# Each product of a split fp32r matmul as two products of 256 moving columns

## The chip, the cores and the metric

The kernel runs on one core of one Trainium2 chip. The core's engines work side by side, each on its own list of instructions: TensorE (PE in the profile, with its weight loads shown apart as PEld), VectorE (DVE), ScalarE (ACT), GpSimd (POOL) and SyncE (SP), which issues most of the DMAs. TensorE writes its results into PSUM, which the kernel uses as eight banks of 128 partitions by 512 fp32 columns. The metric is the device time of one execution in microseconds (us).

## The reference

One input of 2048 rows and 512 columns goes through four layers, each with a residual: a Fourier mixing layer, an attention layer with a compressive memory, and both once more. Cut to what matters:

```python
x = x + _A_ref(_layernorm(x), dft_seq_re, dft_seq_im, dft_hid_re, dft_hid_im)
x = x + _B_ref(_layernorm(x), wq, wk, wv, wo, beta)
x = x + _A_ref(_layernorm(x), ...)
x = x + _B_ref(_layernorm(x), ...)

def _A_ref(x, Cr, Ci, Wr, Wi):        # y = Real(DFT_seq(DFT_hidden(x)))
    a, b = x @ Wr.T, x @ Wi.T
    return Cr @ a - Ci @ b            # Cr, Ci: 2048 x 2048

def _B_ref(x, wq, wk, wv, wo, beta):  # 32 heads of 16, 4 segments of 512 rows
    q, k, v = x @ wq, x @ wk, x @ wv
    for s in range(4):
        p = softmax(q_s @ k_s.T * scale + mask)          # within the segment, causal
        o_s = g * (phi(q_s) @ M) / (phi(q_s) @ z + 1e-6) + (1 - g) * (p @ v_s)
        M, z = M + phi(k_s).T @ v_s, z + sum(phi(k_s))   # memory for later segments
    return o @ wo
```

All of it is fp32 at its inputs and outputs.

## The kernel before

**Split products.** The large matrix products run in fp32r, a form of fp32 on TensorE. To keep their accuracy, each operand is split into two fp32r tensors: `split` (line 95) rounds the source to `hi` (a copy on ACT, line 99, or on DVE, line 97) and stores the rest, source minus `hi`, as `lo` (on DVE or POOL, line 101). A pair of them lies side by side in one tile of 128 x 2 x 512. `matmul3` (line 107) then adds three products into one PSUM bank: hi times hi, hi times lo and lo times hi. Its stationary operand (`lhsT`) has 128 columns, its moving operand (`rhs`) 512, so one product fills a whole bank. `first` and `last` say whether this call opens or closes the accumulation in the bank.

**Where it is used.** Six places call it, and the profile names their results by their banks:

- `contract` (line 306), banks `u`: the first Fourier layer's transform along the rows. For each of 4 blocks of 512 output columns, 16 chunks of 128 rows are accumulated into 8 banks (4 for the real part and 4 for the imaginary one). Stationary is the normalised input `xa`, moving are the split blocks `chi` and `clo` of the DFT matrix.
- `product` (line 333), banks `m`: the same transform in the second Fourier layer, in a form with seven block products instead of eight (`P1` to `P7`), each summed over 8 chunks into two banks.
- `hidden` and `hidden_last` (lines 372 and 391), banks `y`: the transform along the columns in both Fourier layers, with the split result `us` stationary and the split weights `wdt` moving.
- `proj` (line 500), banks `pqk`, and `values` (line 480), banks `pvv`: the projections to q, k and v of the attention.
- `outproj` and `outproj_split` (lines 860 and 889), banks `po`: the output projection.

Every other product of the attention stays outside `matmul3`: `nat` and `sT` are bf16 scores (of a row maximum and of the softmax), `pv_bank` is the product with the values, `pm` and `pM` read and update the memory, `xnT`, `oT`, `on`, `pkT` and `mT` are transposes.

**The order of work.** Each piece of work is a generator. `place` puts its steps on numbered slots, and at the end all slots are run in order, so the program is written out step by step. All PE instructions go through one helper, `in_order` (line 83, the call itself on line 87), which keeps them in program order; that is why the profile gives line 87 for all of them. The other engines' instructions are ordered by the framework's scheduler, which follows the order of the program but lets an instruction under `tc.high_priority(offset=...)` count as if it stood that many instructions earlier. That is used for DVE's row maxima (`natural_max`, line 602, with `URGENT = 150` of line 41; line 618 with twice that) and for ACT's copy of them (line 640). A row maximum is taken by DVE from a bank `nat` into `mx` (line 603); from four of them come `parts`, which PE transposes (`mT`), and which a DMA then writes into the stack of queries that the products `sT` read.

In the attention stages, runs of a few `matmul3` products stand between the scores of one unit and the next; in the Fourier stages thousands of them follow each other.

Of the kernel before, what the change touches and what calls it, by code (L numbers as in the profile page):

```python
# [61 lines left out]
def spectral_infini_kernel(  # L62
# [13 lines left out]
    V, A, G, T = nc.vector, nc.scalar, nc.gpsimd, nc.tensor  # L76
# [6 lines left out]
    def in_order(engine, name):  # L83
        op = getattr(engine, name)

        def call(*args, **kwargs):
            return tc.keep_in_program_order(op(*args, **kwargs))  # L87

        return call

    T = SimpleNamespace(matmul=in_order(T, "matmul"), transpose=in_order(T, "transpose"))
# [13 lines left out]
            )  # L105

    def matmul3(ps, lhsT, rhs, first, last):
        T.matmul(ps, lhsT(0), rhs(0), start=first, stop=False)
        T.matmul(ps, lhsT(0), rhs(1), start=False, stop=False)
        T.matmul(ps, lhsT(1), rhs(0), start=False, stop=last)  # L110

    def rows(ap, i):
        return ap[i * P : (i + 1) * P, :]
# [76 lines left out]
    def place_spectral(x_in, x_out, t0, end, ln_at, direct):  # L190
# [115 lines left out]
        def contract(tcn):  # L306
            ps = [[bank(f"u{d}") for d in range(DT)] for _ in range(2)]
            for k in range(HALF):
                for h2 in range(2):
                    for cc in range(2):  # L310
                        parts = right[tcn, cc, k]
                        for d in range(DT):
                            matmul3(
                                ps[cc][d],
                                lambda h: xa[k + HALF * h2][:, h, d * P : (d + 1) * P],
                                lambda h: parts[h][:, h2],
                                (k, h2) == (0, 0),
                                (k, h2) == (HALF - 1, 1),
                            )
                        if (k, h2, cc) != (HALF - 1, 1, 1):  # L320
                            yield
            for cc in range(2):
                for d in range(DT):
                    if d % 2 == 0:
                        block(tcn, (d // 2, cc))
                    dst = c[tcn, (d // 2, cc)][:, d % 2]
                    if cc == 0:
                        A.activation(dst, ps[cc][d], AF.Copy)
                    else:
                        V.tensor_scalar(dst, ps[cc][d], -1.0, None, op0=ALU.mult)  # L330
            yield

        def product(tcn, name):
            ps = [bank(f"m{m}") for m in range(2)]
            for k in range(HALF):
                t = right[tcn, name, k]
                for m in range(2):
                    matmul3(
                        ps[m],
                        lambda h: left(name, k, h, m),  # L340
                        lambda h: t[:, h],
                        k == 0,
                        k == HALF - 1,
                    )
                if k < HALF - 1:
                    yield
            for j, base, _ in TERMS[name]:
                if base != j:
                    block(tcn, j)
            for m in range(2):  # L350
                for j, base, op in TERMS[name]:
                    dst = c[tcn, j][:, m]
                    if base is None:
                        A.activation(dst, ps[m], AF.Copy)
                    else:
                        V.tensor_tensor(out=dst, in0=c[tcn, base][:, m], in1=ps[m], op=op)
            yield
# [14 lines left out]
        def hidden(tcn):  # L372
            for tt in range(LT):
                ps = bank("y")
                xr = load_rows(x_in[tcn * LT + tt], "xr")
                for cc in range(2):
                    for d in range(DT):
                        ut, w = us[tcn, tt, cc], wdt[cc, d]
                        matmul3(
                            ps,  # L380
                            lambda h: ut[:, h, d * P : (d + 1) * P],
                            lambda h: w[:, h, :],
                            (cc, d) == (0, 0),
                            (cc, d) == (1, DT - 1),
                        )
                        if (cc, d) != (1, DT - 1):
                            yield
                finish(ps, xr, x_out, tcn * LT + tt)
                yield
# [712 lines left out]
```

## Time and profile before

| | |
|---|---|
| device time, median of 3 runs | 1908.67 us (1908.55 to 1909.09) |
| span of the profiled execution | 1911.1 us |
| PE: busy, matmuls | 1809.7 us (95% of the span), 10336 |
| PEld: busy, weight loads | 1301.0 us (68%), 10336 |
| DVE busy | 1311.1 us (69%) |
| ACT busy | 1062.9 us (56%) |
| POOL busy | 512.5 us (27%) |
| mean granted TensorE clock | 0.985 |

The profiled execution's own time is its span, 2.4 us above the median of the runs. By time it falls into the first Fourier layer (to about 470 us), the first attention layer (to about 980), the second Fourier layer (to about 1400) and the second attention layer; neighbouring layers overlap a little at each border.

How the profile is read: the span runs from the first instruction to the last. Busy time of an engine is the time in which at least one of its instructions runs. For PE that includes the time from a matmul's issue to its last result, and since matmuls overlap each other, the durations of single ones add up to more than the busy time. A row of a group of instructions names the line, engine, operation, tile written and tiles read, shapes and count; then the busy time and the mean duration of one in ns; then the idle time of the engine just before them, and after whom it ended. In the timeline, a row is the start in us from the span's start, the length in us, and how many equal instructions follow each other in it. Matmul rows name the active rows and columns of the array (`128*128`) and then the moving operand (`128x512`).

### The profile page before, as it was taken

The numbers are of one execution on the slowest core, as the hardware profiler recorded it, in microseconds if no ns is written. First come the engines' busy times: TensorE is split into PE (matmuls) and PEld (weight loads), VectorE is DVE, ScalarE is ACT, GpSimd is POOL, SyncE is SP. The second block draws the span as 40 slices with busy tenths as digits, with TensorE's granted clock in tenths as the row PEclk, the third lists the DMA queues.
The fourth block names the chain that finished last, engine by engine and source line by source line (L and its number), as shares of the span: only waits on it lengthen the run. The fifth ranks groups of instructions, "written<-read, shape, count | busy, mean of one in ns | idle before, by whom it ended". The sixth has DMA issues, their size and how long they took to land. (4 is left out here: it accounts for less than half of the span.)

```text
span 1911.1 us, 31877 instructions
## 1 busy us (share of the span) xinstructions
PE 1809.7 (95%) x10336; PEld 1301.0 (68%) x10336; DVE 1311.1 (69%) x4073; ACT 1062.9 (56%) x2292; POOL 512.5 (27%) x831
## 2 busy tenths in 40 slices
PE   7899999999899999999889999999988999999998
PEld 6678888888556656665458888787865655666654
DVE  8654545462787787777866687777558778777773
ACT  3221213331578777767664465453337877777775
POOL 4200000002345344446431000000124443434432
PEclk9999999999899999999999999999999999999998
DMA  6665555353544333434445787563444434444231
GB/s 224 233 208 199 189 191 198 115 173 121 178 125 148 118 120 115 149 119 134 134 154 181 222 251 225 164 204 127 159 150 139 144 108 134 126 133 142 91 117 45
DMA packets 165655, 296.49 MB, mean 155 GB/s; under 512 B 17776, under 2 KB 66928, under 8 KB 165488
## 3 DMA queue, kind: packets, MB, share of 16 engines
q1 hardware_dynamic: 162224, 293.68, 47.5%
q8 instruction: 81, 1.33, 0.3%
q10 hardware_dynamic: 3264, 0.79, 0.2%
q14 instruction: 86, 0.70, 0.1%
HBM read 192.95 MB, written 100.66 MB: 154 GB/s over the span
## 5 line engine op out<-in xcount | busy, mean ns | idle before, releaser
L603 DVE CUSTOM_DVE_ANT_0 junk<-nat,mask 128x512 bf16<-128x512 f32 (+3 forms) x1024 | 496.6, 485 | 203.2 <-PE nat L87 183.9
L669 ACT ACTIVATE pT<-sT 128x512 f32<-128x512 f32 x640 | 370.3, 598 | 15.0 <-ACT sT L668 2.2
L87 PE MATMUL u<-chi,xa 128*128 128x512 f32 x1024 | 321.1, 395 | 10.9 <-DVE xa L97 7.3
L672 POOL TENSOR_SCALAR_AFFINE_SELECT pT<-pT 128x256 f32<-128x256 f32 (+1 forms) x448 | 197.4, 455 | 431.5 <-ACT pT L669 366.8
L87 PE MATMUL sT<-stkq,stkk 99*128 99x256 bf16 (+3 forms) x1024 | 250.7, 307 | 17.5 <-DVE mx L603 8.8
L87 PE MATMUL nat<-stkk,stkq 96*128 96x512 bf16 (+3 forms) x1024 | 246.5, 302 | 20.8 <-DVE mx L603 12.4
L668 ACT ACTIVATE sT<-sT 128x256 f32<-128x256 f32 (+1 forms) x640 | 208.6, 334 | 63.9 <-PE sT L87 56.7
L87 PEld LDWEIGHTS u<-chi,xa 128*128 128x128 f32 x1024 | 195.4, 191 | 52.8 <-issue 7.2
L87 PE MATMUL u<-clo,xa 128*128 128x512 f32 x512 | 202.6, 396 | 9.6 <-DVE clo L101 9.6
L142 POOL TENSOR_TENSOR r<-ve,half_neg 128x2 f32<-128x2 f32 (+1 forms) x33 | 24.0, 728 | 696.5 <-DVE ve L140 692.9
L87 PE MATMUL y<-wdt,us 128*128 128x512 f32 x768 | 182.5, 391 | 1.2 <-DVE wdt L101 1.2
L87 PEld LDWEIGHTS <-stkk 99*128 99x128 bf16 x1024 | 82.6, 99 | 146.3 <-issue 127.9
L87 PEld LDWEIGHTS y<-wdt,us 128*128 128x128 f32 x768 | 143.4, 188 | 31.6 <-DVE wdt L101 2.0
L87 PE MATMUL pv_bank<-pT,vt 128*17 128x128 f32 (+3 forms) x2048 | 158.7, 440 | 1.7 <-POOL pT L672 1.6
L87 PEld LDWEIGHTS <-stkq 96*128 96x128 bf16 x1024 | 94.9, 99 | 75.9 <-issue 37.3
L87 PE MATMUL po<-wo,oh 128*128 128x512 f32 x384 | 125.7, 443 | 7.6 <-DVE oh L101 5.4
L87 PE MATMUL pvv<-wv,xT 128*128 128x512 f32 x384 | 127.0, 443 | 3.9 <-DVE mx L603 3.9
L87 PE MATMUL pqk<-xT,wq 128*128 128x512 f32 x384 | 129.9, 447 | 0.0
L87 PE MATMUL pqk<-xT,wk 128*128 128x512 f32 x384 | 127.8, 442 | 0.0
L87 PEld LDWEIGHTS u<-clo,xa 128*128 128x128 f32 x512 | 97.7, 191 | 32.5 <-DVE clo L101 12.2
L87 PEld LDWEIGHTS pv_bank<-pT,vt 128*17 128x17 f32 x2048 | 57.6, 98 | 90.7 <-issue 77.0
L99 ACT ACTIVATE clo<-cring 128x512 fp32r<-128x512 f32 x112 | 70.6, 631 | 69.1 <-DVE chi L101 37.9
(138 smaller groups left out, 3032.0 us busy)
## 6 DMA issues: line engine op xcount, KB each, us to landing
sum<-sring SPq DMA_DIRECT2D x32, 1024.0 KB
cring<-sum SPq DMA_DIRECT2D x128, 256.0 KB
stkq<-scrq SPq DMA_DIRECT2D x64, 384.0 KB
stkk<-scrk SPq DMA_DIRECT2D x64, 384.0 KB
cring<-in_ct SPq DMA_DIRECT2D x96, 256.0 KB
sring<-in_ct SPq DMA_DIRECT2D x32, 512.0 KB
xt<-mid SPq DMA_DIRECT2D x64, 256.0 KB
craw<-in_ct SPq DMA_DIRECT2D x30, 512.0 KB
```

The costliest lines, as they stand in the source:

```text
L87: return tc.keep_in_program_order(op(*args, **kwargs))
L99: A.activation(hi, src, AF.Copy, scale=scale)
L142: G.tensor_tensor(out=r, in0=ve, in1=half_neg[:, :n], op=ALU.pow)
L603: V.tensor_tensor_reduce(junk[:, :n], src, mask[:, 512 - n :], 1.0, 3e38, ALU.add, ALU.min, dst,)
L668: A.activation(blocks, blocks, AF.Relu)
L669: A.activation(dst, ps, AF.Exp, scale=-SCALE)
L672: G.affine_select(blocks, blocks, pattern=[[0, n] for n in blocks.shape[1:-1]] + [[1, P]], compare_op=ALU.is_ge, fill=0.0, base=0, channel ...
```

## The change

`matmul3` issues each of its three products twice: once on the moving columns 0 to 255 into the first half of the bank, and once on the columns 256 to 511 into its second half, with the same stationary operand. Only the very first product in a bank opens the accumulation, and both halves of the last term close it. Everything else in the program's text is as before; lines below `matmul3` are numbered 8 higher.

```diff
     def matmul3(ps, lhsT, rhs, first, last):
-        T.matmul(ps, lhsT(0), rhs(0), start=first, stop=False)
-        T.matmul(ps, lhsT(0), rhs(1), start=False, stop=False)
-        T.matmul(ps, lhsT(1), rhs(0), start=False, stop=last)
+        terms = (0, 0), (0, 1), (1, 0)
+        for a, b in terms:
+            for c in 0, 256:
+                T.matmul(
+                    ps[:, c : c + 256],
+                    lhsT(a),
+                    rhs(b)[:, c : c + 256],
+                    start=first and (a, b, c) == (0, 0, 0),
+                    stop=last and (a, b) == terms[-1],
+                    skip_group_check=True,
+                )
```

## The prediction

> **What bounds the kernel now.** I read the page first: its line of the span, its table of busy time and its table of DMA queues.
>
> ```profile
> span 1911.1 us, 31877 instructions
> ...
> PE 1809.7 (95%) x10336; PEld 1301.0 (68%) x10336; DVE 1311.1 (69%) x4073; ACT 1062.9 (56%) x2292; POOL 512.5 (27%) x831
> ...
> q8 instruction: 81, 1.33, 0.3%
> ...
> q14 instruction: 86, 0.70, 0.1%
> ```
>
> TensorE (PE) is busy 95% of the span and no other engine passes 69%. A busy share alone does not say where PE sets the pace, so next come the windows by stage. The columns are the window, its length, then busy time and instructions of PE, PEld, DVE, ACT and POOL, then granted clock, DMA share and GB/s.
>
> ```profile
> 0.00:130.00 130.00, 109.48 (x442) 87.32 (x443) 90.89 (x171) 34.72 (x44) 35.07 (x41) 0.96 0.66 224
> 130.00:470.00 340.00, 340.00 (x1510) 281.48 (x1509) 169.58 (x263) 92.06 (x151) 10.91 (x10) 1.00 0.52 175
> 470.00:980.00 510.00, 470.95 (x3223) 295.43 (x3222) 393.43 (x1594) 368.73 (x865) 231.79 (x384) 0.97 0.42 132
> 980.00:1400.00 420.00, 415.40 (x1866) 338.66 (x1865) 284.15 (x514) 198.78 (x364) 25.15 (x28) 1.00 0.59 188
> 1400.00:1911.00 511.00, 473.82 (x3303) 298.12 (x3301) 373.07 (x1533) 368.61 (x869) 209.62 (x369) 0.98 0.38 121
> ```
>
> The spectral stages (130 to 470, 980 to 1400) leave PE idle 0 and 4.6 us. The attention stages leave 39.1 and 37.2 us, the first 130 us leave 20.5. So a time added to each product of a spectral stage reaches the end in full, and in the other stages nearly so. The longest of the waits in the third window is this (total, times, longest):
>
> ```profile
> PE nat L87 <- DVE mx L603: 6.7, 12, 1.6
> ```
>
> It is a loop: DVE takes a maximum of what PE has just made, and PE waits for the bank. Slower products elsewhere on PE give DVE more time for it, but I credit nothing for that.
>
> The products that the change touches are these groups, by form. The columns are names and shapes, count, busy time and mean ns of one, then idle time before.
>
> ```profile
> L87 PE MATMUL u<-chi,xa 128*128 128x512 f32 x1024 | 321.1, 395 | 10.9 <-DVE xa L97 7.3 <-ACT chi L99 3.3 <-POOL xa L101 0.4
> L87 PE MATMUL u<-clo,xa 128*128 128x512 f32 x512 | 202.6, 396 | 9.6 <-DVE clo L101 9.6
> L87 PE MATMUL y<-wdt,us 128*128 128x512 f32 x768 | 182.5, 391 | 1.2 <-DVE wdt L101 1.2
> L87 PE MATMUL pqk<-xT,wq 128*128 128x512 f32 x384 | 129.9, 447 | 0.0
> L87 PE MATMUL pqk<-xT,wk 128*128 128x512 f32 x384 | 127.8, 442 | 0.0
> L87 PE MATMUL pvv<-wv,xT 128*128 128x512 f32 x384 | 127.0, 443 | 3.9 <-DVE mx L603 3.9
> L87 PE MATMUL po<-wo,oh 128*128 128x512 f32 x384 | 125.7, 443 | 7.6 <-DVE oh L101 5.4 <-DVE mx L603 0.9 <-ACT oh L99 0.7
> L87 PE MATMUL m<-chi,xa 128*128 128x512 f32 x384 | 99.8, 396 | 0.0
> L87 PE MATMUL m<-clo,xa 128*128 128x512 f32 x384 | 99.3, 394 | 0.0
> L87 PE MATMUL m<-clo,xb 128*128 128x512 f32 x192 | 49.6, 391 | 1.8 <-DVE clo L101 1.8
> L87 PE MATMUL m<-chi,xb 128*128 128x512 f32 x192 | 48.7, 389 | 0.0
> L87 PE MATMUL m<-chi,xs 128*128 128x512 f32 x96 | 25.1, 393 | 0.0
> L87 PE MATMUL m<-clo,xs 128*128 128x512 f32 x96 | 24.4, 389 | 0.0
> ```
>
> The counts add up to 1536 (u) + 768 (y) + 768 (pqk) + 384 (pvv) + 384 (po) + 1344 (m) = 5184 products. The mean of one (389 to 447 ns) is a latency and not a price, since products overlap. The price is the distance from start to start, read where nothing but such products runs (window, length, busy time and count of PE, granted clock, DMA):
>
> ```profile
> 150.00:350.00 200.00, 200.00 (x884) 1.00 0.56 192
> 55.70:59.50 3.80, 3.80 (x11) 0.50 0.39 126
> ```
>
> The first row gives 200.00 / 884 = 0.2262 us for a product, at a granted clock of 1.00; 5184 of them are 1173 us, 61% of the span. The second is a stretch at clock 0.50, and the timeline there (start, length, count) shows:
>
> ```profile
> 55.61 1.05 PE L87 MATMUL u<-chi,xa 128*128 128x512 f32 x2
> ...
> 58.17 1.05 PE L87 MATMUL u<-chi,xa 128*128 128x512 f32 x2
> ```
>
> Six products start between 55.61 and 58.17 (two, one, two and one, by the three rows left out): 2.56 / 6 = 0.427 us each. Half of that is 0.2133, so at full clock a product takes 0.0129 us more than its array time. At half clock nothing of this excess is left, which is how a supply of moving data that is a little too slow at full clock behaves (it would grow with the columns). But a fixed time for each instruction that a longer product hides would also look so. What the change costs hangs on which of the two it is.
>
> **The change part by part.** It replaces each of 5184 products by two with 256 moving columns, and adds 5184 products and, if none is shared, 5184 weight loads. PE's order is the old one with each product doubled. No wait, transfer, tile or DMA issue is added or removed.
>
> *The products.* No fp32r product of 256 columns stands in the trace, so the price is bounded by rows. The lower end: array time alone, 0.1067 each, would be 0.2133 a product, a gain of 0.0129; the weight loads raise that end (below). The upper end: the whole excess for each half, 0.1067 + 0.0129 = 0.1196, or 0.2391 a product. Between them stand two near rows, of like length and with one weight load each:
>
> ```profile
> 1770.68 0.39 PE L87 MATMUL sT<-stkq,stkk 99*128 99x512 bf16 x1
> 1770.90 0.38 PE L87 MATMUL nat<-stkk,stkq 96*128 96x256 bf16 x2
> ```
>
> ```profile
> 1775.51 0.39 PE L87 MATMUL sT<-stkq,stkk 99*128 99x256 bf16 x2
> 1775.74 0.38 PE L87 MATMUL nat<-stkk,stkq 96*128 96x512 bf16 x1
> ```
>
> The sT pair is this very form in bf16, two products of 256 columns in the halves of one bank: 1775.74 - 1775.51 = 0.23 us, against 1770.90 - 1770.68 = 0.22 for one of 512. The pM products are as long as a half and load weights of the same size (the timeline, then the groups):
>
> ```profile
> 529.52 1.09 PE L87 MATMUL pM<-vt,pkn 128*128 128x136 f32 x8
> ```
>
> ```profile
> L87 PE MATMUL pM<-vt,pkn 128*128 128x136 f32 x192 | 26.7, 282 | 4.9 <-DVE mx L603 4.9
> ...
> L87 PEld LDWEIGHTS pM<-vt,pkn 128*128 128x128 f32 x192 | 24.9, 189 | 7.3 <-ACT sT L668 5.3 <-ACT pT L669 1.1
> ```
>
> Eight in 1.09 us, with the last one's 0.28 taken off, are 0.81 / 7 = 0.116 each. I take 0.1155 for a half, 0.231 for a product, since both rows (0.230 and 0.232 a pair) lie there. That is 0.231 - 0.2262 = +0.0048 us, times 5184 = +24.9 us.
>
> *The weight loads.* Each now has 0.1155 us of product to hide under instead of 0.2262. One load takes 0.19 us from issue to end, but pM shows loads of 189 ns under products 0.116 apart, so loads overlap each other's latency. How close they can stand:
>
> ```profile
> 24.37 0.30 PEld L87 LDWEIGHTS u<-chi,xa 128*128 128x128 f32 x2 [0.85 <-POOL xa L101]
> ```
>
> Two in 0.30 us, the last of them 0.19 long, are 0.11 apart. That is the floor of a half, 0.22 a product (a gain of 0.0062, the lower end kept), and leaves some 5 ns of cover at 0.1155. I cost them at nothing. If the cover is gone by 5 ns a half, it is 2 x 0.005 x 5184 = +52 us, within the upper end of the products.
>
> The Trainium skill (TensorE: Matmul & The Clock Gate, "LDWEIGHTS") puts a load of 128 columns at 128 / 1.2 = 107 ns. The two loads 0.11 us apart agree. By that figure a half would stay at or above 107 ns, which speaks against any large gain.
>
> *Instruction fetch.* Queue q8 holds 1.33 of 1.33 + 0.70 = 2.03 MB of instructions, 66%, as PE and PEld hold 20672 of 31877; it is PE's. 10368 more instructions are 41 packets more. A packet takes 0.3% x 16 x 1911 / 81 = 1.1 us, and 122 instead of 81 make one in 16 us instead of 24. Prefetch hides it; if it hid nothing, +45 us. I take 0.
>
> *Order on other engines.* DVE, ACT, POOL and SP keep their instructions; some move by a few places, because the urgency of DVE's maxima is an offset counted in instructions (URGENT = 150) and now reaches over fewer steps. The bound is the idle PE of the attention stages, 39.1 + 37.2 = 76 us: a third of it more or less is 25 us either way. I take 0.
>
> *Cover in the first 130 us.* Part of PE's 20.5 idle us there is waiting for split inputs, which a slower PE meets later: I take -1 us for its 442 products (442 x 0.0048 = 2.1, half of it).
>
> **Sum.** 24.9 - 1 = +24, so a span of 1911.1 + 24 = 1935 us. The median of the runs, 1908.67, lies 2.4 below the profiled span, so 1932.7, and I say 1933 us, +1.3%. Anything within 0.2% (3.8 us) counts as no change.
>
> **The rivals.**
>
> *The excess belongs to the instruction.* Each half carries 0.0129: +0.0129 x 5184 = +67, with the same -1 us some 1975; with some 10 us more for the shortened cover, 1985. For it: the excess is the same in 884 products in a row, whatever they read. Against it: none of it is left at half clock.
>
> *The other side: the excess is not paid by a short product.* It would have to arise beyond the 256th column; then a half runs as fast as its weight load permits, 0.11, and the kernel gains 0.0062 x 5184 = 32 us: 1877. It decides as soon as a half falls below 0.1131. For it: sT's 512 columns at 0.22 show that 512 columns need not cost 0.226. Against it: the sT pair is slower than one of 512, and pM, with a load of this size, stands at 0.116.
>
> The Trainium skill (same page, "Back-to-back issue gap") gives 518 cycles for 512 columns and 262 for 256 at 2.4 GHz: 216 and 109 ns. By it a pair would take 218 ns, and against the 226 measured here the change would gain 0.0079 x 5184 = 41 us, 1868. Its 216 fits sT's 0.22 and not the fp32r products' 0.226, so I give its side little weight.
>
> *A weight load doesn't fit under a half.* If the products waited for the whole 0.19 us of each load, a product would take 0.38: +0.15 x 5184 = +800 us, 2710. pM speaks against it. A narrow product could also run in a slower form; no row shows one.
>
> *The pair shares one load.* The time would be as forecast, loads being hidden, but PEld would stay near x10336. Against it: the first two products of each three already have one stationary operand, and there are as many loads as products (x10336 each).
>
> **How the numbers follow.** Forecast (a half between 0.1135 and 0.118, 1912 to 1960 us): 0.46. Excess per instruction, with reordering or fetch on top, 1960 to 1990: 0.29. No change: 0.05. Faster: 0.14. Worse than 1990, weight loads above all: 0.06. The range 1905 to 1990 leaves out about 2 in 10, the faster runs and the worst; faster 0.14, same 0.05, slower 0.81.
>
> **What would show it.** Right: PE at about 15520 matmuls and as many loads, windows of a spectral stage with 0.115 us a product, its stages longer by 2% (130 to 470 becoming some 347 us) and PE still without idle there. If the window shows 0.120, the excess is the instruction's; 0.110, the loads set the pace; 0.113, supply alone. The idle PE of the attention stages should stay near 76 us; if it grows by 20 or more, the order of DVE's work matters and I was wrong to cost it at nothing. Doubled latency of q8 packets with idle PE "from issue" would blame the fetch. I am wrong altogether if fp32r products of 256 columns have a rate of their own.

## The result and the profile after

The changed kernel takes 1953.81 us (median; 1944.17 to 1955.68) beside 1908.61 us for the kernel before: 1.0235 times as long, 95% interval 1.0216 to 1.0254. The forecast was 1933, with a range of 1905 to 1990.

The page of the changed kernel begins with its span and the busy times:

```profile
span 1954.0 us, 42263 instructions
...
PE 1859.8 (95%) x15520; PEld 1632.4 (84%) x15520; DVE 1301.8 (67%) x4073; ACT 1062.1 (54%) x2292; POOL 511.3 (26%) x831
...
q8 instruction: 122, 2.00, 0.4%
```

Every product is doubled (10336 + 5184 = 15520) and so is its weight load: nothing is shared within a pair. PE is as full as before, and PEld went from 68% to 84% of the span. The other engines' busy times are what they were.

The rate is in the window from 150 to 350 us, where only these products run. Columns: window, length, then busy time and count of PE, PEld, DVE, ACT and POOL, then granted clock, DMA share, GB/s.

```profile
150.00:350.00 200.00, 200.00 (x1669) 200.00 (x1669) 97.80 (x128) 46.93 (x59) 0.00 (x0) 1.00 0.54 182
```

200.00 / 1669 = 0.1198 us for a half, 0.240 for a product that took 0.2262 before. Such a count also holds the products that reach over the two ends of the window, so these quotients come out up to 0.2% low. The timeline of the kernel before gives the whole product more closely, with three of them from 360.15 to 360.83, 0.2267 each; by their start times the halves stand 0.1200 apart:

```profile
360.15 0.62 PE L87 MATMUL u<-chi,xa 128*128 128x512 f32 x2
360.60 0.39 PE L87 MATMUL u<-clo,xa 128*128 128x512 f32 x1
360.83 0.62 PE L87 MATMUL u<-chi,xa 128*128 128x512 f32 x2
```

The weight loads are busy for all 200 us of the window, where before (the row below) they were for 165.6 of them:

```profile
150.00:350.00 200.00, 200.00 (x884) 165.59 (x883) 103.25 (x135) 49.57 (x62) 0.00 (x0) 1.00 0.56 192
```

The timeline of PEld after the change shows how they stand:

```profile
358.98 0.55 PEld L87 LDWEIGHTS u<-chi,xa 128*128 128x128 f32 x4
359.46 0.31 PEld L87 LDWEIGHTS u<-clo,xa 128*128 128x128 f32 x2
359.70 0.55 PEld L87 LDWEIGHTS u<-chi,xa 128*128 128x128 f32 x4
```

Six loads start from 358.98 to 359.70, 0.120 apart, each still running when the next one starts. By the start times in the trace (medians of the window), a load starts 0.003 us after a product has started, and the load's own product 0.117 us after the load. At granted clock 0.50 nothing is lost, as in the kernel before (four halves in 0.85 us, 0.213 each, where a whole product took 0.427):

```profile
57.61 1.05 PE L87 MATMUL u<-chi,xa 128*128 128x256 f32 x4
58.46 0.63 PE L87 MATMUL u<-clo,xa 128*128 128x256 f32 x2
58.89 1.05 PE L87 MATMUL u<-chi,xa 128*128 128x256 f32 x4
```

Where the time came from shows when both executions are cut at the same products (the last `y` and the first `m` of each layer). First before, then after:

```profile
0.00:484.00 484.00, 463.48 (x2014) 379.32 (x2014) 266.52 (x453) 128.64 (x198) 50.71 (x55) 0.99 0.55 184
484.00:969.70 485.70, 446.65 (x3103) 278.49 (x3101) 381.94 (x1561) 360.99 (x849) 223.06 (x376) 0.97 0.42 133
969.70:1411.20 441.50, 436.90 (x1973) 353.67 (x1972) 294.08 (x540) 206.52 (x380) 33.87 (x36) 0.99 0.58 185
1411.20:1911.10 499.90, 462.62 (x3252) 289.54 (x3251) 368.58 (x1519) 366.75 (x866) 204.89 (x365) 0.98 0.39 122
```

```profile
0.00:504.90 504.90, 487.03 (x4003) 485.03 (x4003) 268.06 (x453) 128.51 (x198) 51.83 (x55) 0.99 0.54 177
504.90:991.90 487.00, 447.63 (x3755) 339.26 (x3753) 376.09 (x1561) 361.12 (x850) 222.38 (x376) 0.97 0.43 132
991.90:1455.30 463.40, 459.92 (x3819) 454.34 (x3817) 293.30 (x540) 205.66 (x379) 33.62 (x35) 0.99 0.58 177
1455.30:1954.00 498.70, 465.22 (x3952) 353.76 (x3950) 364.36 (x1519) 366.79 (x866) 203.52 (x365) 0.98 0.40 123
```

The Fourier stages grew by 20.9 and 21.9 us, the attention stages by 1.3 and -1.2. All but 0.1 of the 42.9 us lies in the Fourier stages, where such products set the pace, although the attention stages gained some 650 and 700 products each.

### The profile page after: what moved, and what is told of

It reads as the page before. It is cut to its first block, busy times and chain, and to the rows that moved or that the text cites. A ratio compares the mean times of both kernels' runs of the same rounds, so it can differ in the third digit from the quotient of the medians.

```text
span 1954.0 us, 42263 instructions
## 1 busy us (share of the span) xinstructions
PE 1859.8 (95%) x15520; PEld 1632.4 (84%) x15520; DVE 1301.8 (67%) x4073; ACT 1062.1 (54%) x2292; POOL 511.3 (26%) x831
## 4 chain that ended last, share of the span: by engine, by line
PE 77%; DVE 11%; issue 4%; DMA 4%; ACT 2%; POOL 1%; SPq 0%; DVEq 0%; ACTq 0%; POOLq 0%
PE u L87 16%; PE m L87 15%; PE y L87 8%; PE pqk L87 7%; PE pv_bank L87 6%; PE sT L87 6%; PE nat L87 5%; DVE junk L611 4%; PE pvv L87 4%; PE po L87 4%; DMA xt<-mid 2%; PE on L87 1%; PE pM L87 1%; PE pm L87 1%; DVE sring L304 1%
## 5 line engine op out<-in xcount | busy, mean ns | idle before, releaser
L87 PE MATMUL u<-chi,xa 128*128 128x256 f32 x2048 | 333.3, 285 | 9.1 <-DVE xa L97 7.6
L87 PEld LDWEIGHTS u<-chi,xa 128*128 128x128 f32 x2048 | 286.1, 194 | 9.4 <-issue 7.6
L87 PE MATMUL u<-clo,xa 128*128 128x256 f32 x1024 | 209.1, 286 | 8.8 <-DVE clo L101 8.8
L87 PE MATMUL y<-wdt,us 128*128 128x256 f32 x1536 | 192.2, 284 | 0.8 <-DVE wdt L101 0.8
L87 PEld LDWEIGHTS u<-clo,xa 128*128 128x128 f32 x1024 | 161.5, 194 | 10.1 <-DVE clo L101 10.1
L87 PE MATMUL pqk<-xT,wq 128*128 128x256 f32 x768 | 134.4, 312 | 0.5 <-ACT vt L504 0.5
L87 PE MATMUL po<-wo,oh 128*128 128x256 f32 x768 | 127.3, 306 | 6.8 <-DVE oh L101 4.2
L87 PE MATMUL pvv<-wv,xT 128*128 128x256 f32 x768 | 131.3, 311 | 2.1 <-DVE mx L611 2.1
L87 PE MATMUL pqk<-xT,wk 128*128 128x256 f32 x768 | 126.8, 302 | 0.0
L87 PEld LDWEIGHTS po<-wo,oh 128*128 128x128 f32 x768 | 105.7, 194 | 18.9 <-DVE oh L101 9.8
```

## The experiments

The trace after leaves two readings of 0.120. The array time of 512 columns at full clock is 0.2133 us, half of the 0.427 measured at clock 0.50, so 2.4 columns pass in a ns. By the first reading, each fp32r instruction carries 0.0133 us beside its columns: 256 / 2.4 + 13.3 = 120 ns, and 512 / 2.4 + 13.3 = 226.7. By the second, the columns come at 17/16 of the array's time (226.7 for 512, 113.3 for 256), and a half waits for its weight load at 120. Both give the same two numbers. The experiments had to part them, and to say why the attention stages paid next to nothing.

**Only the Fourier layers split, only the attention split.** `matmul3` gets a flag that the calls in the attention set.

```diff
+    def matmul3(ps, lhsT, rhs, first, last, attention=False):
+        cuts = ((0, 256), (256, 256)) if attention == False else ((0, 512),)
```

(`attention == True` in the other kernel.)

> Only the Fourier layers' products (u, m, y: 3648) are split, the attention's stay at 512 columns. Theory P (the fixed cost of an fp32r instruction, 0.0133 us at full clock, is paid once more for each product, and PE never waits in these layers): 3648 x 0.0133 = 48 us, less what half clock and the input waits of the first 130 us give back, so +38 to +46 us, about 1950. Rival Q (the measured +45 us spread evenly over all products): 45 x 3648 / 5184 = +32 us, about 1940.

> Only the attention's products (pqk, pvv, po: 1536) are split. Theory P with what the short runs of the kernel before show (about 0.232 us a product there and not 0.2267, so a split adds only some 0.005 to 0.007): +4 to +11 us, 1913 to 1920. Rival Q (even spread): +13 us, 1922. If the order of DVE's maxima cost something, it would show here as more PE idle and +20 us or more.

Splitting the Fourier layers alone gave 1.0239 (1.0205 to 1.0274), the whole of the loss. Splitting the attention alone gave 1.0008 (0.9987 to 1.0029): no change. So the even spread (Q) is refuted, and theory P was near for the Fourier layers (medians 1952.8 against 1907.9, +45). For the attention it expected 4 to 11 us, and the medians differ by +0.7; the interval, -2.5 to +5.5 us, leaves only the lower end of that open. One short run of products in the attention, before and after, shows why little is added there. First before, then after, the same instructions:

```profile
1770.68 0.39 PE L87 MATMUL sT<-stkq,stkk 99*128 99x512 bf16 x1
1770.90 0.38 PE L87 MATMUL nat<-stkk,stkq 96*128 96x256 bf16 x2
1771.04 0.94 PE L87 MATMUL pvv<-wv,xT 128*128 128x512 f32 x3
1771.83 0.39 PE L87 MATMUL sT<-stkq,stkk 99*128 99x512 bf16 x1
```

```profile
1816.12 0.39 PE L87 MATMUL sT<-stkq,stkk 99*128 99x512 bf16 x1
1816.35 0.39 PE L87 MATMUL nat<-stkk,stkq 96*128 96x256 bf16 x2
1816.48 0.96 PE L87 MATMUL pvv<-wv,xT 128*128 128x256 f32 x6
1817.28 0.39 PE L87 MATMUL sT<-stkq,stkk 99*128 99x512 bf16 x1
```

From sT to sT the start times in the trace give 1.150 us before and 1.165 after: 0.005 for a product, and not 0.013. The first of the three takes 0.320 before and 0.319 after. Its load starts only 0.024 us ahead of it in both, so nothing covers that load, and the split adds nothing. The other two go from 0.232 and 0.230 to 0.241 and 0.240. The 467 runs of three in the traces of the kernel before and of the attention split, paired in order, grew by a median of 0.016 us, 5.7 us in all. Why the median of the runs shows even less can't be told from a single execution; PE's waits may have taken up a part.

**The three terms inside, the halves outside.** Neighbours no longer alternate between the halves of the bank.

```diff
-        for a, b in terms:
-            for c in 0, 256:
+        for c in 0, 256:
+            for a, b in terms:
```

> The same six products, but all three terms of the first half of the bank before those of the second, so that two neighbours no longer share a stationary operand in pairs and no longer alternate between the halves. If the cost belongs to each instruction: 0.120 us a product in the window from 150 to 350 us, time as the changed kernel (1944 to 1956). If it comes from going back and forth between the halves of a bank: below 0.115 a half and 20 us or more faster than the changed kernel. If from loading the same weights twice: about the same in the hi-hi and hi-lo terms, so no change either.

1.0213 (1.0188 to 1.0237), and 200.00 us for 1669 halves in the window, as in the changed kernel. The order of halves and of shared stationary operands has no part in it.

**384 and 128 columns.**

```diff
-            for c in 0, 256:
+            for c, n in ((0, 384), (384, 128)):
```

> Each product as 384 and 128 columns. The law that 512 and 256 give (0.0133 us and one column in 1/2.4 ns): the 384 takes 0.1733. For the 128 the law alone gives 0.0667; the weight load, which two in a row show at 0.11, would hold it at 0.107 to 0.11; a load that needs a handover of its own, 0.120. So a pair is 0.240, 0.280 to 0.283 or 0.293. With 5184 products against 0.2267: +69, +277 to +292, or +344 us.

1.151 (1.1463 to 1.1557), some 289 us more. The timeline:

```profile
300.02 0.74 PE L87 MATMUL u<-chi,xa 128*128 128x384 f32 x4
300.60 0.45 PE L87 MATMUL u<-clo,xa 128*128 128x384 f32 x2
300.88 0.74 PE L87 MATMUL u<-chi,xa 128*128 128x384 f32 x4
```

Three products in 0.86 us, 0.287 each, between the 0.283 and the 0.293 expected. So a short product is held back by the load beside it; from this alone the two readings can't be told apart, since 0.170 + 0.117 and 0.173 + 0.113 both fit. The loads start 0.109 and 0.178 us apart in turn, so 0.120 is not the closest that two such loads come while products run.

**Shorter weight loads.** Some terms load only 64 stationary columns, and so fill half of the partitions.

```diff
         for a, b in terms:
+            n = 64 if (a, b) == (0, 1) else P
...
-                    ps[:, c : c + 256],
-                    lhsT(a),
+                    ps[:n, c : c + 256],
+                    lhsT(a)[:, :n],
```

> As the changed kernel, but the hi-lo term loads 64 stationary columns instead of 128 and so fills half of the partitions (the other half of that term is left out). Two of six loads are half as long. If the product's fixed cost doesn't depend on the load: 0.120 a half still, time as the changed kernel. If a half is set by its load of 128 columns and a handover: the two short loads give 0.107 to 0.109 instead of 0.120, a mean of 0.116 in the window, and 20 to 40 us faster.

In the second kernel it is `n = P if (a, b) == (0, 0) else 64`.

> As the changed kernel, but the hi-lo and the lo-hi term load 64 stationary columns (half of each of these terms is left out), so four of six loads are short. If a half is the longer of 0.1133 (its columns) and 0.120 (a load of 128 columns with its handover): (2 x 0.120 + 4 x 0.1133) / 6 = 0.1156 a half in the window from 150 to 350, after 0.1178 with two short loads. If the load doesn't matter: 0.120.

The first gave 1.0128 (1.0092 to 1.0164), about 18 us less than the changed kernel; the second 1925 us in a single run. Their windows, one after the other:

```profile
150.00:350.00 200.00, 200.00 (x1701) 200.00 (x1700) 99.85 (x131) 47.04 (x59) 0.00 (x0) 1.00 0.55 186
```

```profile
150.00:350.00 200.00, 200.00 (x1733) 200.00 (x1732) 101.36 (x133) 48.06 (x60) 0.00 (x0) 1.00 0.57 191
```

0.1176 and 0.1154 us a half, where the second reading gives (4 x 120 + 2 x 113.3) / 6 = 117.8 and (2 x 120 + 4 x 113.3) / 6 = 115.6. The expectation for the first kernel had 0.116, since it put the products with short loads at 0.107 to 0.109; by the second reading their columns hold them at 0.1133. The products still have 256 moving columns in fp32r. With a cost of each instruction they would have stayed at 0.120. So the half of the changed kernel is as long as its weight load permits, and without it would take 0.1133, half of a whole product. The sum of the first reading was right and its mechanism wrong. These two kernels alone leave one doubt: a product with 64 stationary columns also writes only 64 partitions, and might be shorter for that. The next experiment has short loads beside products that write all 128.

**bf16 read from the same tiles.** The operands are the upper halves of the fp32r numbers, so the columns still lie 4 bytes apart; the lower bits are left out of the products.

```diff
-                    lhsT(a),
-                    rhs(b)[:, c : c + 256],
+                    lhsT(a).bitcast(BF16)[:, 1::2],
+                    rhs(b).bitcast(BF16)[:, 1::2][:, c : c + 512],
```

(`c + 256` in the second kernel.)

> All split products read the upper half of each fp32r number as bf16 (every second 2-byte element of the same tiles), 512 columns, one instruction a product, as in the kernel before; this leaves the lower bits out of both operands. If the fixed cost belongs to the fp32r form: 0.2153 to 0.220 us a product in the window 150 to 350 (the bf16 products sT take 0.22), some 30 to 56 us faster than before. If every matmul of 512 columns with such operands pays it: 0.2267, no change.

> The same in bf16, each product as two of 256 columns. If the fixed cost belongs to the fp32r form: 0.108 to 0.110 a half, within 15 us of the run with 512 bf16 columns. If splitting costs the same in every form: 0.120 a half, some 45 us slower than the run with 512 bf16 columns.

With 512 columns 0.9884 (0.9855 to 0.9912), with 256 0.9908 (0.9879 to 0.9937), and 4.6 us between their medians. The windows of the two, 512 first (of its matmuls some records are missing; its 882 loads count the products):

```profile
150.00:350.00 200.00, 198.81 (x866) 84.67 (x882) 103.12 (x135) 49.64 (x62) 0.00 (x0) 1.00 0.57 192
```

```profile
150.00:350.00 200.00, 200.00 (x1767) 169.41 (x1766) 104.13 (x137) 48.61 (x61) 0.00 (x0) 1.00 0.57 191
```

200.00 / 882 = 0.2268 and 200.00 / 1767 = 0.1132. For 512 columns the second price expected came out, without its "no change" in time; for a half neither 0.108 to 0.110 nor 0.120 did. The excess is there in bf16 too, so it isn't a cost of the fp32r form. And it halves with the columns, so it isn't a cost of the instruction. With short bf16 loads (0.10 us from issue to end) a half of 256 columns and all 128 partitions takes 0.1133, which puts what fp32r pays above that on its load, and the split itself is almost free. The 22 us that the kernel with 512 columns gains on the one before, at the same 0.2267 in the long runs, lie mostly in the attention stages, which are 9.5 and 10.6 us shorter in the profiled executions. That they come from the shorter loads at the head of each short run is possible but wasn't tried alone.

**One column read 512 times.** fp32r, unsplit, with step zero in the moving operand; the other 511 columns are left out.

```diff
-        T.matmul(ps, lhsT(0), rhs(0), start=first, stop=False)
...
+            T.matmul(
+                ps,
+                lhsT(a),
+                rhs(b)[:, :1].to_broadcast([P, 512]),
```

> fp32r, 512 columns, one instruction a product as in the kernel before, but the moving operand is its first column read 512 times (step zero), so the result is left out of it. If the 0.0133 us come from how many different bytes are read: 0.2153 to 0.217. If they belong to the fp32r form, whatever it reads: 0.2267.

```profile
150.00:350.00 200.00, 200.00 (x925) 174.86 (x925) 107.00 (x140) 51.20 (x64) 0.00 (x0) 1.00 0.59 197
```

The single run took 1868 us. 200.00 / 925 = 0.2162: nearly all of the excess is gone, with the same form and the same loads. It belongs to the reading of moving columns that lie 4 bytes apart.

**Both parts stored as bf16.** The kernel before, with `hi` and `lo` rounded to bf16 and stored without gaps. What that costs in accuracy beside two fp32r parts was not measured here.

```diff
-    def pair(name, tag, bufs, dtype=F32R):
+    def pair(name, tag, bufs, dtype=BF16):
...
-        lo_engine.tensor_tensor(out=lo, in0=src, in1=hi.bitcast(F32), op=ALU.subtract)
+        lo_engine.tensor_tensor(out=lo, in0=src, in1=hi, op=ALU.subtract)
...
-                    xT[s] = sb.tile([P, 2, DT, 512], F32R, name="xT", bufs=1)
+                    xT[s] = sb.tile([P, 2, DT, 512], BF16, name="xT", bufs=1)
```

> The kernel before with hi and lo stored as bf16 (rounded, and the rest rounded), side by side without gaps, 512 columns a product; the accuracy is that of two bf16 parts instead of two fp32r parts. If the 0.0133 us of a product come from reading moving columns 4 bytes apart (both fp32r and every second bf16 element took 0.2267 for 512): 0.2153 to 0.217 in the window from 150 to 350, and in all 0.011 x 5184 = 57 us less than the run that read every second element (1889), so 1830 to 1850. If they come from the accumulation in one bank: 0.2267 and about 1889.

> The same with each product as two of 256 columns. Columns close together: 0.108 to 0.109 a half, within 15 us of the run with 512. If the change itself (two halves of a bank) had a price of its own beside reading and loading, it would be seen here as more than 0.110 a half.

Unsplit 0.9724 (0.9695 to 0.9753), 1857 us: it beats both kernels. Split 0.976 (0.9737 to 0.9782). Their windows, unsplit first (counted by its 927 loads):

```profile
150.00:350.00 200.00, 199.00 (x910) 90.67 (x927) 105.26 (x138) 51.70 (x65) 0.00 (x0) 1.00 0.58 195
```

```profile
150.00:350.00 200.00, 200.00 (x1834) 179.26 (x1833) 104.42 (x136) 52.08 (x65) 0.00 (x0) 1.00 0.57 193
```

0.2157 for 512 columns and 0.1091 for 256: the excess is gone when columns lie 2 bytes apart, and two halves cost 0.0025 us more than a whole, 3648 of which are 9 us (6.5 between the medians). Beside these 0.0025 the halves of a bank have no price of their own. The total came out at 1857 and not at 1830 to 1850. In the long runs the gain per product was as expected, and against the run with every second element the Fourier stages are 20.5 and 14.0 us shorter. But the attention stages, where 1536 x 0.011 = 17 us were counted on, are 1.0 and 3.1 us longer: PE is busy there 4.1 us less and idle 8.2 us more, in one execution of each kernel.

## Why the prediction was right, and which of its terms was mis-sized

The direction and the range held, and so did one reason: PE sets the pace in the Fourier stages, and what a product costs more there reaches the end nearly in full. The point was short by half (+24 forecast, +45 measured), because a half was priced too low. That the time still fell between 1912 and 1960 us, the band of the prediction's main case, is partly luck: that band stood for halves of 0.1135 to 0.118. At 0.120 for all 5184 products its own sum would have given 0.0133 x 5184 = 69 us, and the attention's products did not pay that. The parts of the sum:

- **The price of a half** was put at 0.1155, from rows of other forms, and is 0.120. That is 0.0133 a product and not 0.0048. The bf16 pair, "this very form", has short loads. The pM products (136 columns of fp32, 0.116 apart) spend about two columns' time on each column, as the transposes `xnT`, `on` and `pkT` do (128 columns, 0.109), so they need never have waited for a load. Neither row has what meets here. The 0.22 read for one sT of 512 is a difference of rounded times: the start times in the trace give 0.229, so that row did not speak for less than 0.226.
- **The weight loads** were costed at nothing, with "some 5 ns of cover at 0.1155". This is the step that failed. The 0.11 came from two loads in a row on an idle PE; beside products of 256 columns they stand 0.120 apart, and the products wait for them. The bound given for it ("if the cover is gone by 5 ns a half", +52 us) was the size of what happened. Why a product follows its load by 0.117 us here, when loads also come 0.109 apart in the kernel of 384 and 128 columns, stays open.
- **The excess of 0.0129** (0.0133 by the timeline) was left open between two causes, and the first of them holds: a supply of moving data that is a little too slow at full clock. The bf16 runs and the one with a single column show it: it grows with the columns and goes away when they lie close. Of itself it would have made the change free (0.1133 a half).
- **The attention's products** were charged 0.0048 each like the others, 1536 x 0.0048 = 7 us. The traces show 5.7 us in their short runs, the times of whole runs +0.7 (-2.5 to +5.5). The Fourier stages account for the rest: 3648 x 0.0133 = 48.5, of which they show 42.8. PE's idle time in them fell by 3.8 us (25.1 to 21.4 by the windows above); the last 2 us were not taken apart.
- **The first 130 us** gave back 2.6 us of PE's idle time (112.13 us busy after, 109.48 before) where 1 was credited.
- **Instruction fetch** and **the order on other engines** were costed at nothing, and no cost of theirs shows: q8 has the 122 packets foretold, and the attention stages leave PE idle 39.4 and 33.5 us by the windows above, 39.1 and 37.3 before.
- **The rivals.** The excess of each instruction gave the right price of a half (0.1196) for a wrong reason, and a time (1975) as far off as the forecast, since it charged the attention too. The sign set for it, a window at 0.120, did not tell it from the load: both give 0.120. The other side fell, because no fp32r half came near 0.11. The rule of the Trainium skill (TensorE: Matmul & The Clock Gate, "Back-to-back issue gap"), 216 and 109 ns, is what the bf16 parts without gaps show (0.2157 and 0.1091) and not what fp32r shows (0.2267 and 0.120). Giving it little weight was right by the fp32r rows.

## What to carry to other kernels

In this kernel a product met three limits: its columns in the array (0.2133 us for 512), the reading of its moving operand (0.2267), and the next weight load (0.120 a half). Which of them binds can change when the product gets shorter, so a price read from a long one says nothing of half of it: look in the trace for how close two weight loads of that size stand while products run. The price from a long run did not hold in runs of three either: the split cost 0.005 us a product there, and 0.0133 in the long ones. Where fp32r is used only for accuracy by splitting, ask whether bf16 parts do: here they took away both the slow reading and the long loads.

## What the runs showed of the hardware

- Moving columns 4 bytes apart took 0.2267 us for 512, in fp32r and as every second bf16 element, and 0.1133 for 256 as bf16, at full clock: 17/16 of the array's time. Columns 2 bytes apart took 0.2157 and 0.1091, one column repeated 0.2162. At granted clock 0.50 nothing was lost.
- fp32r weight loads of 128 columns with products of 256 columns between them stood 0.120 us apart (a product followed its load by 0.117); with 64 columns in some of the loads the mean fell to 0.1176 and 0.1154.
- The two products of one stationary operand, next to each other, never shared a load: 15520 products, 15520 loads.
